# Sliding-window attention scores: 128-key triangles in four quarters of 32 keys on sixteen 32x32 array tiles, in place of two halves of 64 keys on eight 32x64 tiles

## The chip, the cores and the metric

The kernel runs on one core of one Trainium2 chip. The metric is the device time of one execution in microseconds (us). Several executions of each kernel are timed.

## The reference, cut to what matters

```python
def _A_ref(x, wqkv, wo):             # x: 2048 x 1024, 32 heads of 32, window 256
    ...
    scores = jnp.einsum("bhqd,bhkd->bhqk", q, k) * (Dh ** -0.5)
    mask = (idx[:, None] - idx[None, :] >= 0) & (idx[:, None] - idx[None, :] < W)
    scores = jnp.where(mask[None, None], scores, -1e9)
    p = _softmax(scores, axis=-1)
    o = jnp.einsum("bhqk,bhkd->bhqd", p, v)
    ...
h = x + _A_ref(_layernorm(x, axis=-1), A_wqkv, A_wo)
h2 = h + _B_ref(_layernorm(h, axis=-1), B_w1, B_w2)   # dense, SiLU, dense
```

A query sees its own key and the 255 before it. In tiles of 128 keys this gives, for each key tile, one triangle on the diagonal, one full tile, and one triangle at the far end of the window.

## The kernel before

The sequence goes through in four blocks of 512 queries, the heads in eight groups of four. The score work of a block is cut into *bursts*, placed between dense matmuls of the next block (or of the output projection) so that the tensor engine (PE) need not wait (it is busy for 99% of the span). A burst fills the four score banks of PSUM, the memory that PE writes to; ScalarE takes the exponential out of them, GpSimd clears the masked corners, and later PE multiplies by V. An X or Y burst holds, for one group of heads, four triangles (two of the key tile in its middle, one of each of two other key tiles) and one full piece; a C burst holds only full 128-key pieces, which need no mask. A block has 16 X/Y bursts and 4 C bursts.

```python
    def scores_xy(b, g, odd):
        q0 = odd * P
        mid, first, last = odd, odd - 2, odd + 2
        parts = [                                   # key tile, 64-key half, query from, to, bank column
            (mid, 0, q0, q0 + 320, 64), (mid, 1, q0 + 64, q0 + 384, 128),
            (last, 0, q0 + 256, q0 + 384, 384), (first, 1, q0, q0 + 128, 0),
            (first, 0, q0, q0 + 64, 0), (last, 1, q0 + 320, q0 + 384, 448),
        ]
        for step in range(3):
            for hh in range(4):
                for kt, half, qa, qb, col in parts[step * 2:step * 2 + 2]:
                    ...
                    nc.tensor.matmul(
                        sc[hh // 2][half * 64:half * 64 + 64, hh % 2, col:col + qb - qa],
                        lhsT=kT[t // 4][r0:r0 + DH, g, k0:k0 + 64],
                        rhs=qT[b][r0:r0 + DH, g, qa:qb],
                        start=True, stop=True, tile_position=(r0, half * 64),
                    )
        ...                                         # per pair of heads: two exponentials, two selects

    class Stream:
        def __init__(self, b):
            ...
            for g in range(0, G, 2):
                self.bursts += [lambda g=g: scores_c(b, g)]
                self.bursts += [lambda g=g, k=k, o=o: scores_xy(b, g + k, o) for k in range(2) for o in range(2)]
        def between(self, kt):                      # called ahead of each of a block's 192 dense matmuls
            if self.seen * 20 >= self.done * 192:
                self.bursts[self.done]()
                self.done += 1
            ...
```

Each `nc.tensor.matmul` is two instructions of the tensor engine, a weight load and a matmul (the page counts 5859 of each). An X/Y burst has 24 of them, so 48 instructions, in three waves of eight: 320 columns, then 128, then 64 on each 32x64 tile.

The softmax here doesn't subtract the row's maximum and nothing guards it: scores larger than these inputs give would overflow.

## Time and profile before

| | before |
|---|---|
| median of 4 runs | 693.75 us (693.42 to 694.03) |
| span in the profile | 691.9 us |
| PE busy | 99% |
| X/Y burst, cost on PE | 452 ns, 48 of them |
| C burst, cost on PE | 430 ns, 12 of them |
| PE instructions, load and matmul | 11718 |

The cost of a burst is the time from the last dense matmul before it to the first after it, less one dense spacing of 215.5 ns. It is a better figure than "busy", which is 100% in these blocks (58.00 of 58.00 us from 106.00 on), because the records of matmuls overlap: that of a dense one lasts 379 ns, and the next starts after 215.5. The lines that carry these numbers are in the prediction below.

### The profile page before, as it was taken

The numbers are of one execution on the slowest core, as the hardware profiler recorded it, in microseconds if no ns is written. First come the engines' busy times: TensorE is split into PE (matmuls) and PEld (weight loads), VectorE is DVE, ScalarE is ACT, GpSimd is POOL, SyncE is SP. The second block draws the span as 40 slices with busy tenths as digits, with TensorE's granted clock in tenths as the row PEclk, the third lists the DMA queues.
The fourth block names the chain that finished last, engine by engine and source line by source line (L and its number), as shares of the span: only waits on it lengthen the run. The fifth ranks groups of instructions, "written<-read, shape, count | busy, mean of one in ns | idle before, by whom it ended". The sixth has DMA issues, their size and how long they took to land.

```text
span 691.9 us, 13823 instructions
## 1 busy us (share of the span) xinstructions
PE 687.3 (99%) x5859; PEld 330.1 (48%) x5859; DVE 292.5 (42%) x616; ACT 240.8 (35%) x400; POOL 161.8 (23%) x295
## 2 busy tenths in 40 slices
PE   8999999999999999999999999999999999999998
PEld 3444445555555555544444444444444444444445
DVE  6267646744444449543315133343133251333111
ACT  4326656666766676521310033300133100233000
POOL 1007666656666665500000000000000000000000
PEclk9999999999999999999999999999999999999999
DMA  7732231236462999971023410023200023100110
GB/s 243 259 60 72 33 93 54 26 63 174 81 131 18 228 248 276 228 267 46 16 76 109 98 38 1 1 91 70 84 0 1 17 94 94 39 1 1 30 39 24
DMA packets 76462, 60.93 MB, mean 88 GB/s; under 512 B 50288, under 2 KB 60528, under 8 KB 76400
## 3 DMA queue, kind: packets, MB, share of 16 engines
q1 hardware_dynamic: 76256, 59.78, 33.1%
q8 instruction: 46, 0.75, 0.5%
q10 hardware_dynamic: 144, 0.26, 0.1%
q14 instruction: 16, 0.13, 0.1%
HBM read 39.85 MB, written 8.39 MB: 70 GB/s over the span
## 4 chain that ended last, share of the span: by engine, by line
PE 99%; DMA 0%; DVE 0%; issue 0%
PE hacc L615 19%; PE hacc L652 17%; PE acc L250 16%; PE acc L652 10%; PE acc L615 9%; PE acc L240 8%; PE acc L271 7%; PE o_ps L377 4%; PE sc L302 3%; PE hacc L271 1%; PE o_ps L392 1%; PE sc L348 1%; PE sc L328 1%; DMA r_o<-in_A_x_dram 0%; PE tp L218 0%; DVE ln_st L171 0%
## 5 line engine op out<-in xcount | busy, mean ns | idle before, releaser
L368 POOL TENSOR_SCALAR_AFFINE_SELECT r_e<-r_e 128x512 bf16<-128x512 bf16 (+1 forms) x288 | 158.8, 570 | 125.7 <-ACT r_e L357 64.7
L652 PEld LDWEIGHTS <-r_a 128*128 128x128 bf16 x952 | 90.9, 98 | 103.0
L615 PEld LDWEIGHTS <-r_w 128*128 128x128 bf16 x896 | 87.5, 98 | 105.0
L652 PE MATMUL hacc<-r_a 128*128 128x512 bf16 (+2 forms) x616 | 122.5, 360 | 0.0
L615 PE MATMUL hacc<-r_e,r_w 128*128 128x512 bf16 x456 | 100.9, 379 | 0.0
L314 ACT ACTIVATE r_e<-sc 128x768 bf16<-128x768 f32 x96 | 78.2, 814 | 48.3 <-PE sc L302 48.3
L624 ACT ACTIVATE r_n<-hacc 128x512 f32<-128x512 f32 x30 | 17.9, 597 | 178.9 <-PE hacc L615 178.9
L652 PE MATMUL acc<-r_a 128*128 128x512 bf16 x336 | 74.0, 379 | 0.0
L250 PEld LDWEIGHTS <-r_w 128*128 128x128 bf16 x512 | 45.0, 97 | 47.3 <-issue 0.2
L252 DVE CAST r_a<-acc 128x512 bf16<-128x512 f32 x56 | 38.6, 690 | 57.1 <-PE acc L250 56.9
L250 PE MATMUL acc<-r_t,r_w 128*128 128x512 bf16 x256 | 61.7, 379 | 0.0
L250 PE MATMUL acc<-r_w 128*128 128x512 bf16 x256 | 59.9, 379 | 0.0
L271 PE MATMUL acc<-r_o,r_a 128*128 128x512 bf16 x208 | 51.9, 379 | 0.0
L615 PE MATMUL acc<-r_e,r_w 128*128 128x512 bf16 x216 | 49.1, 379 | 0.0
L377 PEld LDWEIGHTS <-r_e 128*128 128x128 bf16 x1152 | 37.8, 96 | 14.2
L357 ACT ACTIVATE r_e<-sc 128x1024 bf16<-128x1024 f32 x36 | 34.9, 1021 | 21.2 <-PE sc L348 20.1
L377 PE MATMUL o_ps<-r_a,r_e 128*128 128x33 bf16 x1152 | 38.3, 178 | 0.0
L667 DVE SCALAR_TENSOR_TENSOR r_t<-hacc,r_t 128x512 bf16<-128x512 f32 (+2 forms) x22 | 14.0, 635 | 56.4 <-PE hacc L652 56.4
L315 ACT ACTIVATE r_e<-sc 128x256 bf16<-128x256 f32 x96 | 37.4, 390 | 0.0
L667 DVE SCALAR_TENSOR_TENSOR r_t<-acc,r_t 128x512 bf16<-128x512 f32 x12 | 8.3, 691 | 64.2 <-PE acc L652 64.2
L625 DVE SCALAR_TENSOR_TENSOR r_a<-r_n,hacc 128x512 bf16<-128x512 f32 x30 | 20.6, 688 | 33.0 <-ACT r_n L624 33.0
L615 PE MATMUL hacc<-r_a,r_w 128*128 128x512 bf16 x144 | 32.9, 379 | 0.0
(75 smaller groups left out, 529.0 us busy)
## 6 DMA issues: line engine op xcount, KB each, us to landing
r_w<-in_B_w_dram SPq DMA_DIRECT2D x8, 896.0 KB, 5.5
r_a<-in_B_w_dram SPq DMA_DIRECT2D x7, 1024.0 KB, 7.8
r_w<-in_A_wqkv_dram SPq DMA_DIRECT2D x6, 1024.0 KB, 8.6
h_dram<-r_t SPq DMA_DIRECT2D x16, 256.0 KB, 3.3
r_t<-h_dram SPq DMA_DIRECT2D x16, 256.0 KB, 2.9
out_dram<-r_t SPq DMA_DIRECT2D x31, 128.0 KB, 1.7
r_o<-in_A_x_dram SPq DMA_DIRECT2D x15, 256.0 KB, 3.6
r_e<-h_dram SPq DMA_DIRECT2D x3, 1024.0 KB, 5.7
```

Source lines behind the costliest of these rows:

```text
L240: nc.tensor.matmul(acc, lhsT=lnT_b[b % 2][:, kt, j * P:(j + 1) * P], rhs=wv[:, kt, c * 512:(c + 1) * 512], start=(kt == 0), stop=(kt == KT ...
L250: nc.tensor.matmul(acc, lhsT=wqk[:, kt, col0:col0 + P], rhs=lnT_b[b % 2][:, kt, :], start=(kt == 0), stop=(kt == KT - 1))
L252: copy(out=(qT, kT)[which][b][:, g, :], in_=acc)
L271: nc.tensor.matmul(acc, lhsT=qT[b][:, g, j * P:(j + 1) * P], rhs=wo[:, g, c * 512:(c + 1) * 512], start=(g == 0), stop=(g == G - 1))
L314: nc.scalar.activation(out=tri[:, :, :, 64:256], in_=both, func=ACT.Exp, scale=scale)
L315: nc.scalar.activation(out=e[:, 1024:1280].rearrange("p (h q) -> p h q", q=P), in_=bank[:, :, 192:320], func=ACT.Exp, scale=scale)
L357: nc.scalar.activation(out=e, in_=sc[pair], func=ACT.Exp, scale=scale)
L368: nc.gpsimd.affine_select(out=dst, in_=src, pattern=[[0, n] for n in dst.shape[1:-1]] + [[sgn, P]], compare_op=ALU.is_ge if upper else ALU ...
L377: nc.tensor.matmul(o_ps[pair][:, qt * 2 + hh, 0:VW], lhsT=chunk_of(i, bank, piece, pair, hh), rhs=v[:, b * 4 + kt, g * 4 + pair * 2 + hh, ...
L615: nc.tensor.matmul(acc, lhsT=w1[:, kt, ft * P:(ft + 1) * P], rhs=ln2T[b][:, kt, :], start=(kt == 0), stop=(kt == KT - 1))
L652: nc.tensor.matmul(acc[:, 0:c1 - c0], lhsT=gT[:, ft, j * P:(j + 1) * P], rhs=w2[ft // 4][:, ft % 4, c0:c1], start=(ft == 0), stop=(ft == F ...
L667: nc.vector.scalar_tensor_tensor(out=t_out[j % 2][:, c0:c1], in0=acc[:, 0:c1 - c0], scalar=0.5, in1=t_in[j % 2][:, c0:c1], op0=ALU.mult, o ...
```

## The change

The intent: cut the triangles into quarters of 32 keys. Two triangles, laid so that one fills the empty half of the other, then need 160 columns of a bank (128 and a skew of 32) in place of 192 (128 and 64), so the two such pairs of a bank leave 64 more columns free. These take half of one full piece, and half of what the C bursts did moves into the X/Y bursts. A block needs 2 C bursts in place of 4, so 18 bursts in place of 20, and each burst has a price beyond its columns: 452 ns for X or Y and 430 for C, where 512 columns of a dense matmul take 215.5. The quarters go to sixteen 32x32 array tiles.

```diff
     def scores_xy(b, g, odd):
-        q0 = odd * P
-        mid, first, last = odd, odd - 2, odd + 2
-        parts = [ ... ]
         for step in range(3):
-            for hh in range(4):
-                for kt, half, qa, qb, col in parts[step * 2:step * 2 + 2]:
+            for k in (range(4), range(4), range(3, -1, -1))[step]:
+                edge = 64 * odd + 32 * (k + 1)
+                kt, q0, col, n = (
+                    (odd, odd * P + 32 * k, edge, 288),
+                    (odd + 2, (odd + 2) * P + 32 * k, edge + 288, 512 - 288 - edge),
+                    (odd - 2, 64 * odd, 0, edge),
+                )[step]
...
+                for hh in range(4):
                     nc.tensor.matmul(
-                        sc[hh // 2][half * 64:half * 64 + 64, hh % 2, col:col + qb - qa],
-                        lhsT=kT[t // 4][r0:r0 + DH, g, k0:k0 + 64],
+                        sc[hh // 2][32 * k:32 * (k + 1), hh % 2, col:col + n],
+                        lhsT=kT[t // 4][r0:r0 + DH, g, k0:k0 + 32],
...
-            nc.scalar.activation(out=tri[:, :, :, 64:256], in_=both, ...)      # 768 elements
+            nc.scalar.activation(out=tri[:, :, :, 96:256], in_=both, ...)      # 640
             nc.scalar.activation(out=e[:, 1024:1280]..., ...)                  # 256
+            nc.scalar.activation(out=c_ring[:, (g + 2) % 4, ...], in_=bank[:, :, half0:half0 + 64], ...)  # 128
...
-    def scores_c(b, g):                   # 16 matmuls of 128 columns, two groups
+    def scores_c(b, g0):                  # 32 matmuls of 64 columns, four groups
...
-            if self.seen * 20 >= self.done * 192:
+            if self.seen * 18 >= self.done * 192:
...
-    obuf = [view(r_n, 512 * i, 4, P) for i in range(3)]
+    obuf = [view(r_n, 512 * i, 4, P) for i in range(2)]
-    c_ring = view(r_e, 0, 3, 4, 256)
+    c_ring = view(r_e, 10240, 4, 4, 256)
```

The rest moves buffers, and gives the attention out in halves of eight units in place of pieces of 8, 8, 5, 6 and 5. An X/Y burst now has 48 matmuls, so 96 instructions, in three waves of sixteen. Each tile still streams 512 columns: 288, then 192 to 96 (X) or 128 to 32 (Y), then the rest.

More of the change, by code (lines that the diff above doesn't have):

```diff
@@ L32 @@
 ]
-SPLIT = [(0, 8), (8, 16), (16, 21), (21, 27), (27, 32)]
 def first_stream(n_groups):
@@ L89 @@
     r_a = big.tile([P, 49664], BF16, name="r_a")
-    r_e = big.tile([P, 13312], BF16, name="r_e")
-    r_n = big.tile([P, 1536], BF16, name="r_n")
+    r_e = big.tile([P, 14336], BF16, name="r_e")
+    r_n = big.tile([P, 1024], BF16, name="r_n")
     ps_tp = tc.tile_pool(name="ps_tp", bufs=1, space=bass.MemoryType.PSUM, reuse_waits="tile")
@@ L126 @@
     ebuf = [view(r_e, 1024 * i, 2, 512) for i in range(12)]
-    c_ring = view(r_e, 0, 3, 4, 256)
-    xy_ring = [r_e[:, 3072 + 1280 * i:3072 + 1280 * (i + 1)] for i in range(8)]
-    obuf = [view(r_n, 512 * i, 4, P) for i in range(3)]
+    c_ring = view(r_e, 10240, 4, 4, 256)
+    xy_ring = [r_e[:, 1280 * i:1280 * (i + 1)] for i in range(8)]
+    obuf = [view(r_n, 512 * i, 4, P) for i in range(2)]
     h_blk = [view(r_a, w2_off + 4096 * 4, 4, D)] + [view(r_e, 8192, 4, D)] * 3
@@ L157 @@
     load_wqkv(0)
-    ident = const.tile([P, P], BF16, name="ident")
-    make_identity(nc, ident[:])
+    ident = view(r_e, 2048, P)
+    make_identity(nc, ident)
     warm = ebuf[0]
@@ L217, in turn_first @@
                 kt = h * 2 + i
-                nc.tensor.transpose(out=tp_ps[h][:, i * P:(i + 1) * P], in_=xt[:, kt * P:(kt + 1) * P], identity=ident[:])
+                nc.tensor.transpose(out=tp_ps[h][:, i * P:(i + 1) * P], in_=xt[:, kt * P:(kt + 1) * P], identity=ident)
             nc.scalar.copy(out=dst[:, h * 2:(h + 1) * 2, j * P:(j + 1) * P],
@@ L280, in chunk_of @@
         if bank == "C":
-            return c_ring[:, (i + 1) % 3, pair * 2 + hh, piece * P:(piece + 1) * P]
+            return c_ring[:, (i + 2) % 4, pair * 2 + hh, piece * P:(piece + 1) * P]
         c0 = 1024 + hh * P if piece == 2 else hh * 512 + (piece - piece // 3) * P
@@ L287, in scores_xy @@
     def scores_xy(b, g, odd):
-        q0 = odd * P
-        mid, first, last = odd, odd - 2, odd + 2
-        parts = [
-            (mid, 0, q0, q0 + 320, 64), (mid, 1, q0 + 64, q0 + 384, 128),
-            (last, 0, q0 + 256, q0 + 384, 384), (first, 1, q0, q0 + 128, 0),
-            (first, 0, q0, q0 + 64, 0), (last, 1, q0 + 320, q0 + 384, 448),
-        ]
-        for step in range(3):
-            for hh in range(4):
-                for kt, half, qa, qb, col in parts[step * 2:step * 2 + 2]:
-                    r0 = hh * DH
-                    t = b * 4 + kt
-                    k0 = (t % 4) * P + half * 64
-                    nc.tensor.matmul(
-                        sc[hh // 2][half * 64:half * 64 + 64, hh % 2, col:col + qb - qa],
-                        lhsT=kT[t // 4][r0:r0 + DH, g, k0:k0 + 64],
-                        rhs=qT[b][r0:r0 + DH, g, qa:qb],
-                        start=True, stop=True, tile_position=(r0, half * 64),
-                    )
@@ L308, in scores_xy @@
-        for pair in range(2):
-            e = xy_ring[((b * G + g) % 2 * 2 + odd) * 2 + pair]
-            tri = e[:, 0:1024].rearrange("p (h c q) -> p h c q", h=2, q=256)
-            bank = sc[pair]
-            both = bank[:, :, 0:192]
-            both = bass.AP(tensor=both.tensor, offset=both.offset, ap=[*both.ap[:2], [320, 2], both.ap[2]])
-            nc.scalar.activation(out=tri[:, :, :, 64:256], in_=both, func=ACT.Exp, scale=scale)
-            nc.scalar.activation(out=e[:, 1024:1280].rearrange("p (h q) -> p h q", q=P), in_=bank[:, :, 192:320], func=ACT.Exp, scale=scale)
-            four = e[:, 0:1024].rearrange("p (c q) -> p c q", q=256)
-            select(four[:, :, 0:P], four[:, :, 64:64 + P], False)
-            select(four[:, :, P:2 * P], four[:, :, P:2 * P], True)
@@ L320, in scores_c @@
-    def scores_c(b, g):
-        s0, s1 = (b * G + g + 1) % 3, (b * G + g + 2) % 3
-        order = (g, g + 1) if s0 < s1 else (g + 1, g)
-        for n, gg in enumerate(order):
-            for m, (kt, q) in enumerate(((-1, 0), (2, 3))):
+        for step in range(3):
+            for k in (range(4), range(4), range(3, -1, -1))[step]:
[5 more added lines that the diff above has]
+                )[step]
@@ L325, in scores_c @@
                 t = b * 4 + kt
+                k0 = (t % 4) * P + 32 * k
                 for hh in range(4):
@@ L328, in scores_c @@
                     nc.tensor.matmul(
-                        sc[hh // 2][:, hh % 2, (n * 2 + m) * P:(n * 2 + m + 1) * P],
-                        lhsT=kT[t // 4][r0:r0 + DH, gg, (t % 4) * P:(t % 4 + 1) * P],
-                        rhs=qT[b][r0:r0 + DH, gg, q * P:(q + 1) * P],
+                        sc[hh // 2][32 * k:32 * (k + 1), hh % 2, col:col + n],
+                        lhsT=kT[t // 4][r0:r0 + DH, g, k0:k0 + 32],
+                        rhs=qT[b][r0:r0 + DH, g, q0:q0 + n],
+                        start=True, stop=True, tile_position=(r0, 32 * k),
+                    )
@@ new lines, in scores_xy @@
+        tri0, full0, half0 = 64 * odd, 64 * odd + 160, 448 * (1 - odd)
+        for pair in range(2):
+            bank = sc[pair]
+            e = xy_ring[((b * G + g) % 2 * 2 + odd) * 2 + pair]
+            tri = e[:, 0:1024].rearrange("p (h c q) -> p h c q", h=2, q=256)
+            both = bank[:, :, tri0:tri0 + 160]
+            both = bass.AP(tensor=both.tensor, offset=both.offset, ap=[*both.ap[:2], [288, 2], both.ap[2]])
+            nc.scalar.activation(out=tri[:, :, :, 96:256], in_=both, func=ACT.Exp, scale=scale)
+            nc.scalar.activation(out=e[:, 1024:1280].rearrange("p (h q) -> p h q", q=P), in_=bank[:, :, full0:full0 + P], func=ACT.Exp, scale=scale)
+            nc.scalar.activation(out=c_ring[:, (g + 2) % 4, pair * 2:pair * 2 + 2, 128 - 64 * odd:192 - 64 * odd],
+                                 in_=bank[:, :, half0:half0 + 64], func=ACT.Exp, scale=scale)
+            four = e[:, 0:1024].rearrange("p (c q) -> p c q", q=256)
+            select(four[:, :, 0:P], four[:, :, 96:96 + P], False)
+            select(four[:, :, P:2 * P], four[:, :, P:2 * P], True)
@@ new lines, in scores_c @@
+    def scores_c(b, g0):
+        for m, (kt, q0) in enumerate(((-1, 0), (2, 3 * P + 64))):
+            t = b * 4 + kt
+            for n in range(4):
+                g = g0 + (n + 2) % 4
+                for hh in range(4):
+                    r0 = hh * DH
+                    nc.tensor.matmul(
+                        sc[hh // 2][:, hh % 2, m * 256 + n * 64:m * 256 + (n + 1) * 64],
+                        lhsT=kT[t // 4][r0:r0 + DH, g, (t % 4) * P:(t % 4 + 1) * P],
+                        rhs=qT[b][r0:r0 + DH, g, q0:q0 + 64],
@@ L332, in scores_c @@
                         start=True, stop=True, tile_position=(r0, 0),
                     )
-        lo, hi = min(s0, s1), max(s0, s1)
         for pair in range(2):
-            nc.scalar.activation(out=c_ring[:, lo:hi + 1:hi - lo, pair * 2:pair * 2 + 2, :],
-                                 in_=sc[pair].rearrange("p h (n q) -> p n h q", q=256), func=ACT.Exp, scale=scale)
+            for m in range(2):
+                nc.scalar.activation(out=c_ring[:, :, pair * 2:pair * 2 + 2, m * 192:m * 192 + 64],
+                                     in_=sc[pair][:, :, m * 256:(m + 1) * 256].rearrange("p h (n q) -> p n h q", q=64),
+                                     func=ACT.Exp, scale=scale)
@@ L405, in attn_norm @@
         nc.vector.tensor_tensor(
-            out=obuf[i % 3][:, :, pair * 64:(pair + 1) * 64].rearrange("p t (h d) -> p t h d", d=DH),
+            out=obuf[i % 2][:, :, pair * 64:(pair + 1) * 64].rearrange("p t (h d) -> p t h d", d=DH),
             in0=o_ps[pair][:, :, 0:DH].rearrange("p (t h) d -> p t h d", h=2),
@@ L413, in attn_transpose, with attn_half @@
         nc.sync.dma_start_transpose(out=qT[b][:, g, :].rearrange("p (t q) -> p t q", q=P),
-                                    in_=obuf[i % 3].rearrange("p t d -> p (t d)"))
-    def attn_piece(b, g, first, last):
-        for k in range(2):
-            a, z = max(first - 16 * k, 0), min(last - 16 * k, 16)
-            if a < z:
-                attn_out(b, g + k, a, z)
-                if z == 16:
-                    late.append(lambda k=k: attn_transpose(b, g + k))
+                                    in_=obuf[i % 2].rearrange("p t d -> p (t d)"))
+    def attn_half(b, g, half):
+        attn_out(b, g, half * 8, half * 8 + 8)
+        if half:
+            late.append(lambda: attn_transpose(b, g))
     class Stream:
         def __init__(self, b):
-            self.b, self.bursts, self.done, self.given, self.seen = b, [], 0, 0, 0
-            for g in range(0, G, 2):
-                self.bursts += [lambda g=g: scores_c(b, g)]
-                self.bursts += [lambda g=g, k=k, o=o: scores_xy(b, g + k, o) for k in range(2) for o in range(2)]
+            self.bursts, self.halves, self.done, self.given, self.seen = [], [], 0, 0, 0
+            for g0 in range(0, G, 4):
+                four = [lambda g=g0 + k, o=o: scores_xy(b, g, o) for k in range(4) for o in range(2)]
+                self.bursts += four[0:2] + [lambda g=g0: scores_c(b, g)] + four[2:]
+                self.halves += [lambda g=g0 + k, o=o: attn_half(b, g, o) for k in range(4) for o in range(2)]
         def between(self, kt):
-            if self.seen * 20 >= self.done * 192:
+            if self.seen * 18 >= self.done * 192:
                 self.bursts[self.done]()
                 self.done += 1
-            if self.seen * 40 >= (self.given * 2 + 1) * 192:
+            if self.seen * 36 >= (self.given * 2 + 1) * 192:
+                if self.given % 9 >= 3:
+                    pending.append(self.halves.pop(0))
                 if pending:
                     pending.pop(0)()
-                coming.append(lambda b=self.b, n=self.given: attn_piece(b, n // 5 * 2, *SPLIT[n % 5]))
-                if len(coming) > 2:
-                    pending.append(coming.pop(0))
+                if self.given % 9 == 8:
+                    pending.extend(self.halves[:2])
+                    del self.halves[:2]
                 self.given += 1
@@ L522 @@
     steps, turns = ln1_steps(2)
-    pending, coming = [], []
+    pending = []
     count = [0, 0]
@@ L599 @@
                 steps.pop(0)()
-    pending += coming
     while steps:
```

## The prediction

The sum came to -2.5 + 0.6 + 0.4 - 0.3 = -1.8 us, so 692.1. From rival B a sum on an assumed 13 ns an instruction came to some 200 ns a burst, about 10 us in all, and so to its 702. The text counts columns at 2.4 a ns (53.3, 133 and 213 ns for 128, 320 and 512). The profile before has this rate: by their records, matmuls of 128 and of 512 columns last 219 and 379 ns (L652), so 384 columns take 160; and dense ones of 512 start 215.5 ns apart. The 2 ns a wave and the 13 ns for the first weights are estimates from it and from the spacings in the text.

> **What bounds the kernel now.** I read the page first, then the stretches of the span by stage, then the timeline around single score bursts, then the trace record by record on the tensor engine.
>
> The page and the stretches say the same thing: the tensor engine (PE) is the bound everywhere. Columns of the stretches: start and end in us, length, then the busy time of each engine with its count of instructions, the granted clock and the DMA share.
>
> ```profile
> PE 687.3 (99%) x5859; PEld 330.1 (48%) x5859; DVE 292.5 (42%) x616; ACT 240.8 (35%) x400; POOL 161.8 (23%) x295
> ...
> PE 99%; DMA 0%; DVE 0%; issue 0%
> ```
>
> ```profile
> 106.00:164.00 58.00, 58.00 (x982) 30.75 (x981) 35.60 (x81) 38.72 (x68) 38.45 (x63) 1.00 0.23 35
> 164.00:224.00 60.00, 60.00 (x1017) 32.02 (x1022) 25.96 (x56) 40.79 (x72) 39.84 (x64) 1.00 0.53 114
> 224.00:288.00 64.00, 64.00 (x1086) 34.27 (x1071) 37.79 (x88) 42.86 (x76) 43.35 (x69) 1.00 0.98 242
> ```
>
> The change touches blocks 1 to 3, about 106 to 291 us. There ScalarE (ACT) is busy for two thirds of the time and GpSimd (POOL) likewise, neither on the path. So what counts is how long PE needs for one score burst, and how many bursts there are. "Busy" cannot tell this, as PE is busy 100% whatever happens. The timeline can: columns are start, length, engine, line, operation, then the count.
>
> ```profile
> 141.24 1.24 PE L250 MATMUL acc<-r_w 128*128 128x512 bf16 x5
> ...
> 142.41 0.29 PEld L302 LDWEIGHTS <-r_a 32*64 32x64 bf16 x24 [0.42 <-issue]
> 142.41 0.43 PE L302 MATMUL sc<-r_a 32*64 32x320 bf16 x24
> 142.77 0.55 PEld L250 LDWEIGHTS <-r_w 128*128 128x128 bf16 x4
> 142.77 1.04 PE L250 MATMUL acc<-r_w 128*128 128x512 bf16 x4
> ```
>
> The dense matmuls start 0.2155 us apart (from the records), so after five that begin at 141.24 the sixth would start at 142.32. It starts at 142.77: a burst of X or Y scores costs 0.45 us. The records split it: 93 ns from the end of the dense stream to the first score matmul, 239 ns from the first score matmul to the last, 120 ns from there to the next dense one. 47 of the 48 such bursts cost 452 or 453 ns. The same reckoning gives 429 to 431 ns for all twelve C bursts, for example this one (dense from 135.41, four of them, so due at 136.27, back at 136.70):
>
> ```profile
> 135.41 1.02 PE L250 MATMUL acc<-r_w 128*128 128x512 bf16 x4
> ...
> 136.36 0.40 PE L328 MATMUL sc<-r_a 32*128 32x128 bf16 x16
> ...
> 136.70 1.25 PE L250 MATMUL acc<-r_w 128*128 128x512 bf16 x5
> ```
>
> One burst, at 114.76, waits for ScalarE to empty the score banks and costs 745 ns, 0.29 us too much; note its weight loads cut in two groups.
>
> ```profile
> 114.76 0.11 PEld L302 LDWEIGHTS <-r_a 32*64 32x64 bf16 x5 [0.42 <-issue]
> 114.76 0.72 PE L302 MATMUL sc<-r_a 32*64 32x320 bf16 x24
> 115.07 0.28 PEld L302 LDWEIGHTS <-r_a 32*64 32x64 bf16 x19 [0.20 <-issue]
> ```
>
> The attention pieces (P times V) cost 25.4 ns a matmul and no entry or exit.
>
> [...]of a burst's 452 ns about 93 are the way in and, by the records, some 90 the way out after the last column. This fixed part is what a dropped burst saves. [...]Here eight tiles of 32x64 start 3.3 ns apart; sixteen are not in this trace. [...]An X/Y burst now is 48 (24 loads, 24 matmuls)[...]. [...]The trace has 814 ns for 768 elements and 390 for 256: 0.828 ns an element plus 178.
>
> **The change, part by part.** *C bursts:* the full 128-key pieces of the C bank lose their middle columns to the X and Y bursts, which gain 64 columns of room. So a block has 2 C bursts in place of 4. Each new one has 32 matmuls of 64 columns in place of 16 of 128, the same 512 columns on each of four row tiles. Eight waves in place of four cost some 2 ns each more (128 columns now come 55 to 57 ns apart, 53.3 of it columns at the full clock), so I take 440 ns. Before 12 x 430 = 5.16 us, after 6 x 440 = 2.64 us: **minus 2.5 us**.
>
> *X/Y bursts:* still 16 a block, with 48 matmuls on sixteen tiles. Per tile the columns are 288 + (224 - edge) + edge = 512; before, 320 + 128 + 64 = 512. So the streaming time, 213 ns, does not fall: quarters only make the triangle's blocks tighter, which buys the 64 columns. What grows is the stagger, sixteen starts in place of eight: 8 x 3.3 = 26 ns more. What shrinks is the wait for the first weights: the first wave now lasts 160 ns for 320 columns (133 ns), so 27 ns go to loading 64 columns; for 32 columns I take 13. Net 26 - 13 = 13 ns, at 48 bursts: **plus 0.6 us**.
>
> *ScalarE:* per burst and pair of heads it now has 768 and 256 elements, then 640, 256 and 128: 708 + 390 + 284 ns from the line above. Six instructions sum to 2.76 us; now four sum to 2.41 and take 2.06 on the clock (139.93 to 141.99), an overlap of 0.116 each, so 2.18 us after. A block's period per burst goes from 57.7 / 20 = 2.9 us to about 3.3, so it hides. Between a C burst and the next one, though, there are ten dense matmuls and no attention piece: 2.155 + 0.44 = 2.6 us from start to start, while the banks come free about 0.2 + 0.36 + 2.06 + 0.05 = 2.67 us after the burst's start (spans and waits as in the bursts of before). That is an estimated wait of 0.07 us six times, **plus 0.4 us**; the 0.29 us wait at 114.76 goes, as X and Y bursts are now 10 or 11 dense matmuls and an attention piece apart: **minus 0.3**.
>
> *POOL, attention, buffers:* the selects are the same 192 of the same size, at a longer period; the 1152 attention matmuls are the same, at no switch cost. Each half of a group comes at least 1.5 periods, some 4.9 us, after its last burst; exponentials and selects need about 3 for the first pair of heads. Output buffers go from three to two. A buffer is written again three slots, 9.9 us, after its last write; its transposing DMA lands 2.3 to 6.2 us after issue. Near 285 us the queue is full of other transposes, so a wait below 1 us could appear there. I count zero.
>
> Sum: -2.5 + 0.6 + 0.4 - 0.3 = -1.8 us, so 692.1; I put the middle at **692.5**, as the risks lie on the slow side.
>
> **The rivals.** *Rival A, four streams of columns don't run at full rate.* The sixteen tiles need four different moving streams per row group, now two. [...]At half rate each burst costs 213 ns more: 48 x 0.213 = 10.2 us, so about 702. [...]I give it 17%.
>
> *Rival B, feeding.* [...]A block now averages 28.8 ns an instruction over 57.7 us, and after the change about 20; the trace only shows that the feed is at least that good. [...]Against: the 1.65 ns between two instructions inside a burst shows how fast the array takes them. I give it 15%.
>
> *Rival C, ScalarE or POOL becomes the bound* through 50% more activations. 2.18 us in a period of 3.3 speaks against; if each burst waited 0.1 us it would be 54 x 0.1 = 5 us, so 697. 5%.
>
> **Range and chances.** The plain sum gives 692.1 with about 1 us either way; A or B alone puts it at 702. Eight in ten: 691.0 to 702.5. Faster by over 2% (below 680) would need more than all the bursts' fixed cost, 1%. Slower by over 2% (above 707.7) needs 290 ns more in every X/Y burst, A and B together: 4%.
>
> **What would show it.** In the new timeline an X/Y burst's cost, reckoned as above, should be 455 to 480 ns, with the sixteen first starts within 55 ns; 650 or more means A or B. A shows as a first wave of about 250 ns and even spacing; B as a first wave of 135 to 150 ns, then a gap before the third. C bursts: 430 to 450 ns, two a block. Weight loads split in two groups by a gap mean a wait for ScalarE. The attention matmuls must stay at 25.4 ns; if not, POOL or the two output buffers hold them.

## The result, and the profile after

The changed kernel takes **702.48 us** (701.53 to 703.15, 4 runs) against 693.75 (693.42 to 694.03, 4 runs). The ratio, the mean time of one kernel's runs over that of the other's of the same rounds (so not quite the ratio of these medians), is 1.0125, 95% interval 1.0108 to 1.0143. That is 1.25% slower, which is clear of noise. Its results are correct. It spreads more than the kernel before: 1.6 us from fastest to slowest, against 0.6.

The page after still shows PE as the whole chain, with a little "issue", time in which PE waited for nothing the profile shows:

```profile
PE 684.6 (98%) x6906; PEld 338.7 (48%) x7011; DVE 292.1 (42%) x616; ACT 236.0 (34%) x496; POOL 161.2 (23%) x295
...
PE 97%; issue 2%; DVE 0%; DMA 0%
```

The timeline around one X burst (start, length, engine, line, operation, count):

```profile
146.07 0.81 PE L251 MATMUL acc<-r_w 128*128 128x512 bf16 x3
...
146.81 0.53 PEld L302 LDWEIGHTS <-r_a 32*32 32x32 bf16 x48 [0.42 <-issue]
146.81 0.63 PE L302 MATMUL sc<-r_a 32*32 32x288 bf16 x48
...
147.37 0.55 PEld L251 LDWEIGHTS <-r_w 128*128 128x128 bf16 x4
147.37 0.82 PE L251 MATMUL acc<-r_w 128*128 128x512 bf16 x2
```

Three dense matmuls from 146.07, so the fourth is due at 146.72; it starts at 147.37. The burst costs 0.65 us in place of 0.45. (In many bursts after, the record of the first dense matmul is missing, though its weight load is there; those were read from the load.) All X bursts cost 651 ns and all Y bursts 677 to 679, but for two X bursts, of 700 and 1118 ns, that waited. A C burst:

```profile
143.68 0.59 PE L251 MATMUL acc<-r_w 128*128 128x512 bf16 x2
144.20 0.29 PEld L330 LDWEIGHTS <-r_a 32*128 32x128 bf16 x32 [0.42 <-issue]
144.21 0.41 PE L330 MATMUL sc<-r_a 32*128 32x64 bf16 x32
144.55 0.55 PEld L251 LDWEIGHTS <-r_w 128*128 128x128 bf16 x4
```

Two dense matmuls from 143.68, the next due at 144.11, back at 144.55: 441 ns, as all six are.

What fills the 651 ns? The stretches below count only the X burst's own line; look at the weight loads (PEld), whose records are 87 ns long:

```profile
146.81:147.09 0.28, 0.28 (x32) 0.28 (x33) 1.00 0.88 207
147.09:147.13 0.04, 0.04 (x32) 0.00 (x0) 1.00 1.29 294
147.13:147.26 0.13, 0.13 (x41) 0.12 (x15) 1.00 1.29 293
```

33 of 48 loads come in the first stretch; then there are none at all; then the last 15. Record by record: counted from the burst's first load, the first wave's sixteen matmuls start within 50 ns of each other in most bursts (3.3 ns apart; 58 in this one), the second wave starts at 135 ns and its last matmul at about 185 (194 in this one), and then nothing starts until **320 ns**. From there loads and matmuls come alternately, one each 4.17 ns, the last matmul at 445. The 33rd load, the 65th instruction of the burst, is the last that comes in time. The tiles are free long before: in this burst the third wave's first tile ends its 96 columns, at 2.4 a ns, 40 ns after it began them, near 224 ns.

Where the time went, from the two profiles (spans 691.9 and 700.1, a difference of 8.2 us):

| term | us |
|---|---|
| X/Y bursts, 48: 22.03 to 32.43 | +10.40 |
| C bursts, 12 to 6: 5.17 to 2.65 | -2.52 |
| two stalls of PE outside bursts (175.04 and 279.27, see the run "shift") | +0.97 |
| earlier start of the score stage (50.57 to 50.08; something in the start-up, not looked into) | -0.50 |
| sum | +8.35 |

The terms sum to 0.17 us more than the spans differ by; that rest was not traced. From the first matmul of the dense half on, the two traces take the same 404.92 us. The attention matmuls stay at 25.4 ns apart.

### The profile page after: what moved, and what is told of

Its sections match the earlier page's. It is cut to its first block, busy times and chain, and to the rows that moved or that the text cites. A ratio compares the mean times of both kernels' runs of the same rounds, so it can differ in the third digit from the quotient of the medians.

```text
span 700.1 us, 16094 instructions
## 1 busy us (share of the span) xinstructions
PE 684.6 (98%) x6906; PEld 338.7 (48%) x7011; DVE 292.1 (42%) x616; ACT 236.0 (34%) x496; POOL 161.2 (23%) x295
## 4 chain that ended last, share of the span: by engine, by line
PE 97%; issue 2%; DVE 0%; DMA 0%
PE hacc L617 18%; PE hacc L654 17%; PE acc L251 16%; PE acc L654 10%; PE acc L617 9%; PE acc L241 8%; PE acc L272 6%; PE o_ps L380 4%; PE sc L302 4%; PE hacc L272 1%; PE o_ps L395 1%; PE sc L351 1%; DMA r_o<-in_A_x_dram 0%; PE tp L219 0%; PE sc L330 0%
## 5 line engine op out<-in xcount | busy, mean ns | idle before, releaser
L315 ACT ACTIVATE r_e<-sc 128x640 bf16<-128x640 f32 x96 | 68.6, 714 | 64.8 <-PE sc L302 57.2
L251 PE MATMUL acc<-r_t,r_w 128*128 128x512 bf16 x237 | 58.0, 379 | 1.8 <-issue 1.3
L251 PE MATMUL acc<-r_w 128*128 128x512 bf16 x241 | 57.1, 379 | 1.6 <-issue 1.3
L272 PE MATMUL acc<-r_o,r_a 128*128 128x512 bf16 x190 | 47.9, 379 | 2.3 <-issue 1.9
L380 PEld LDWEIGHTS <-r_e 128*128 128x128 bf16 x1152 | 36.1, 96 | 11.8 <-issue 0.5
L380 PE MATMUL o_ps<-r_a,r_e 128*128 128x33 bf16 x1152 | 36.6, 178 | 0.4 <-issue 0.4
L302 PEld LDWEIGHTS <-r_a 32*32 32x32 bf16 x2304 | 22.9, 88 | 23.3 <-issue 20.7
```

The lines of the kernel that those rows point to most:

```text
L251: nc.tensor.matmul(acc, lhsT=wqk[:, kt, col0:col0 + P], rhs=lnT_b[b % 2][:, kt, :], start=(kt == 0), stop=(kt == KT - 1))
L272: nc.tensor.matmul(acc, lhsT=qT[b][:, g, j * P:(j + 1) * P], rhs=wo[:, g, c * 512:(c + 1) * 512], start=(g == 0), stop=(g == G - 1))
L302: nc.tensor.matmul(sc[hh // 2][32 * k:32 * (k + 1), hh % 2, col:col + n], lhsT=kT[t // 4][r0:r0 + DH, g, k0:k0 + 32], rhs=qT[b][r0:r0 + DH ...
L315: nc.scalar.activation(out=tri[:, :, :, 96:256], in_=both, func=ACT.Exp, scale=scale)
L380: nc.tensor.matmul(o_ps[pair][:, qt * 2 + hh, 0:VW], lhsT=chunk_of(i, bank, piece, pair, hh), rhs=v[:, b * 4 + kt, g * 4 + pair * 2 + hh, ...
```

## The experiments

**Theory F (feed).** The count of a burst's instructions makes the gap, whatever tiles they run on: up to about the 65th they start in time, and later ones from about 320 ns after the burst's first, one each 4.2 ns, as in the profile after. **Rival Q (quarter tiles).** Something about 32x32 tiles makes the third wave slow by itself: its weights, the mode, or four streams of columns for each row of tiles. The four streams are already answered by the trace: from the first wave's start to the second's start on the same tile there are 133 ns, which is 288 columns at 2.4 per ns (120; the rate agrees with "y_order" below, where 64 columns are 26 ns) and 13 that are left for the first weights. So four streams run at the rate of the other matmuls. What was open was whether the count of instructions or the shape of the tile makes the gap.

### s64, s68, s96: the kernel before, longer bursts

```diff
         # at the end of scores_xy, tiles still 32x64
+        for n in range(8):        # 10 in s68, 24 in s96
+            hh = n // 2 % 4
+            kt, half, qa, qb, col = parts[4 + n % 2]
+            ...                   # the same product again, 32 of its columns
```

The repeats write the same values again, so the result stays correct.

> The kernel before, with the 32x64 tiles kept and eight 32-column score matmuls repeated at the end of each X/Y burst: 64 instructions a burst. [...]F expects no gap here: last matmul 265 to 295 ns after the first, a burst costs 465 to 500 ns. Rival Q (quarter tiles: the third weights of a 32x32 tile are slow in themselves) expects the same.

> As s64 with ten repeats: 68 instructions a burst, still 32x64 tiles. F expects a step: the 33rd matmul not before 318 ns after the burst's start, the last at about 328, a burst 525 to 545 ns. Q expects no step: each of two matmuls more costs 4 to 50 ns in all, the 33rd starts as soon as its tile is free, below 300 ns.

> As s64 with 24 repeats: 96 instructions a burst on 32x64 tiles, as many as the changed kernel has on 32x32. F expects the changed kernel's pattern: matmuls 33 to 48 from 320 ns on, 8.3 ns apart, the last at about 445, a burst 640 to 660 ns. Q expects six even waves, the last matmul at 285 to 400 ns and a burst of 485 to 600 ns.

One burst of each, first s64, then s68, then s96 (L314 is the repeats):

```profile
185.01 0.29 PEld L302 LDWEIGHTS <-r_a 32*64 32x64 bf16 x24 [0.42 <-issue]
...
185.23 0.13 PEld L314 LDWEIGHTS <-r_a 32*64 32x64 bf16 x8
...
185.39 0.76 PEld L240 LDWEIGHTS <-r_t 128*128 128x128 bf16 x5
```

```profile
186.97 0.29 PEld L302 LDWEIGHTS <-r_a 32*64 32x64 bf16 x24 [0.42 <-issue]
...
187.19 0.23 PEld L314 LDWEIGHTS <-r_a 32*64 32x64 bf16 x10
...
187.45 0.55 PEld L240 LDWEIGHTS <-r_t 128*128 128x128 bf16 x4
```

```profile
189.50 0.29 PEld L302 LDWEIGHTS <-r_a 32*64 32x64 bf16 x24 [0.42 <-issue]
...
189.72 0.35 PEld L314 LDWEIGHTS <-r_a 32*64 32x64 bf16 x24
...
190.10 0.55 PEld L240 LDWEIGHTS <-r_t 128*128 128x128 bf16 x4
```

From the burst's first load to the dense matmuls' first load: 0.38, 0.48 and 0.60 us.

| | instructions | 32nd matmul starts | 33rd | last | cost of a burst | one run, us |
|---|---|---|---|---|---|---|
| s64 | 64 | 269 ns | - | 269 ns | 472 ns | 694.88 |
| s68 | 68 | 269 ns | 346 ns | 355 ns | 576 ns | 699.82 |
| s96 | 96 | 269 ns | 347 ns | 472 ns | 692 ns | 705.33 |

Eight matmuls more cost 20 ns; **two more than that cost 104**. The step is there on the old tile shape, so rival Q falls. The times, each of one run beside a run of the kernel before at 693.75, go with it: 48 times 20 ns is 0.9 us (measured 1.1), 48 times 124 is 5.9 (measured 6.1), 48 times 240 is 11.5 (measured 11.6).

Three expectations missed, all on the low side: the 33rd matmul came at 346 ns and not at 320, as in the changed kernel, and the bursts cost 576 ns in s68 (525 to 545 expected) and 692 in s96 (640 to 660). The records explain the 26 ns, which is most of the missing cost, and sharpen the theory. In the changed kernel the first matmul's record ends at 293 ns (288 columns), here at 319 (320 columns, and weights of 64). Both times the 66th instruction comes **27 ns after the recorded end of the burst's first matmul**. A burst of the changed kernel at 115.34 us says the same by itself: its third matmul had to wait for ScalarE and started at 71 ns, not at 9, with its record ending at 349. Four late instructions came from 320 on, and then there was a hole until 376, again 27 ns after that end. What the late ones wait for is not in the trace; what it shows is this distance from the end of a record. F in its sharper form expects the late instructions 27 ns after the first matmul's recorded end, in any burst that is long enough to have some. (The profiler models the ends of matmuls; that the wait follows the first matmul's length is tested in "short_first".)

### split: 64 and 32 instructions in place of 96

```diff
+            if self.seen * 18 >= self.done * 192:
+                self.bursts[self.done]()                        # waves 1 and 2
+                self.tail_at = self.seen + 2
+                ...
+            elif self.seen == self.tail_at:
+                self.bursts[self.done - 1](range(2, 3))         # wave 3, two dense matmuls later
```

> The changed kernel with the third wave of each X/Y burst moved two dense matmuls later: 64 and 32 instructions in place of 96, same tiles, same columns, one more way in and out. F expects the third wave's sixteen matmuls to start within 60 ns of each other (3.3 ns apart, as the first wave), first part about 420 ns, second 260 to 310, together about 700 against 651 to 678 now, so the kernel 1 to 4 us slower than the changed one. Q expects the third wave to stay at 8.3 ns a matmul, 125 ns.

```profile
147.73 0.21 PEld L302 LDWEIGHTS <-r_a 32*32 32x32 bf16 x32 [0.42 <-issue]
147.73 0.39 PE L302 MATMUL sc<-r_a 32*32 32x288 bf16 x32
...
148.59 0.14 PEld L302 LDWEIGHTS <-r_a 32*32 32x32 bf16 x16 [0.42 <-issue]
148.60 0.23 PE L302 MATMUL sc<-r_a 32*32 32x128 bf16 x16
```

The third wave's sixteen matmuls now start within 50 ns, on the very tiles on which they took 125. In a burst of 32 instructions they are as quick as the first wave; this settles Q for the quarter tiles too. But a second way in and out costs what the gap did: from the last dense matmul before to the first after, less three dense spacings, 682 to 692 ns for a plain X burst and 696 to 699 for a plain Y burst. Some 14 bursts cost more, mostly 771 to 776, because their second pair of heads waited for ScalarE to empty the banks. One run took 704.14 us, 1.7 above the changed kernel's median, within the 1 to 4 expected.

### short_first: the same 96 instructions, short matmuls ahead

```diff
-        for step in range(3):
-            for k in (range(4), range(4), range(3, -1, -1))[step]:
+        up, down = range(4), range(3, -1, -1)
+        for piece in (1, 0, 2) if odd else (2, 0, 1):           # shortest piece, middle, the other
+            for k in down if odd else up:
```

> The changed kernel with the pieces of each X/Y burst in another order, the same 48 matmuls and columns: shortest piece first (32, 64, 96, 128 columns), then the 288-column middle, then the rest, longest first. Theory F in its sharper form[...] expects matmul 33 at 205 to 225 ns after the start, as the first matmul now ends near 186, the last at 330 to 350, a burst 550 to 580 ns in place of 651 and 678, and the kernel near 697.5 us. If the late matmuls come at a fixed 320 ns after the burst's start, the last starts at 445 and a burst costs about 670, the kernel near 702.5.

```profile
183.30 1.02 PE L241 MATMUL acc<-r_w,r_t 128*128 128x512 bf16 x4
...
184.25 0.42 PEld L303 LDWEIGHTS <-r_a 32*32 32x32 bf16 x48 [0.42 <-issue]
...
184.73 0.82 PE L241 MATMUL acc<-r_w,r_t 128*128 128x512 bf16 x3
```

The loads take 0.42 us in place of 0.53. The 33rd matmul starts at 212 ns (expected 205 to 225), the last at 337, and a burst costs 571 ns (median of 48) in place of 651 and 678, with the same work in another order. The first matmul's record ends at 186 ns, so the late ones again come some 27 ns after it. A fixed delay of 320 ns is refuted: the late ones start at 212 ns in place of 320, and the end of the first matmul's record moved from 293 to 186. The kernel takes 698.51 us (697.93 to 699.09, 4 runs), ratio to the kernel before 1.0068 (1.0051 to 1.0085): nearly half of the loss is back. (Two stalls of the kind looked at under "shift" stand in this profile too.)

### hybrid: 64 instructions, two shapes of tile

```diff
+        for step in range(2):                                   # outer pieces: sixteen 32x64
+            for hh in range(4):
+                for half in range(2):
+                    edge = 64 * odd + 64 * half + 32
+                    ...                                         # some columns too many for one quarter
+        for k in range(4):                                      # then the middle: sixteen 32x32,
+            ...                                                 # which overwrites those
```

> The changed kernel with 64 instructions in an X/Y burst in place of 96, same results: the two outer pieces as sixteen 32x64 matmuls first, then the middle as sixteen 32x32 that overwrite what the wider ones wrote too much. F expects no gap from feeding. If going from 32x64 to 32x32 drains the array as going from 128x128 does (93 ns), a burst costs 600 to 630 ns and the kernel about 699; if it does not, 500 to 530 ns and about 694.5. Below 504 ns a burst would make it faster than the kernel before.

```profile
184.91 0.15 PEld L301 LDWEIGHTS <-r_a 32*64 32x64 bf16 x16 [0.42 <-issue]
184.91 0.32 PE L301 MATMUL sc<-r_a 32*64 32x192 bf16 x16
...
185.16 0.14 PEld L313 LDWEIGHTS <-r_a 32*32 32x32 bf16 x16
185.16 0.34 PE L313 MATMUL sc<-r_a 32*32 32x288 bf16 x16
...
185.43 0.82 PE L241 MATMUL acc<-r_w,r_t 128*128 128x512 bf16 x3
```

No gap as in s68: the sixteen quarter loads come within 50 ns. But going from one tile shape to the other inside the burst costs time: by the columns, the halves end near 158 ns, and the first quarter starts at 249 to 252, 91 to 95 ns later, as on the way in from the dense matmuls (93). (This wait is what the expectation calls a drain; the traces show its length alone.) A burst costs 617 ns, the kernel 699.06 us (698.43 to 699.57, 4 runs), ratio 1.0074 (1.0059 to 1.0089). Expected were 600 to 630 ns and about 699. A way to keep the quarters' room without the long burst exists, but this wait eats it.

### y_order: what the 27 ns between X and Y bursts are

```diff
+            piece = (0, 2, 1)[step] if odd else step
-            for k in (range(4), range(4), range(3, -1, -1))[step]:
+            for k in (range(4), range(4), range(3, -1, -1))[piece]:
```

> The changed kernel with the second and third pieces of the Y bursts exchanged, so that the late matmuls of a Y burst have 128, 96, 64, 32 columns as those of an X burst do, in place of 192, 160, 128, 96. If the late matmuls' own columns lie bare at the burst's end, Y bursts fall from 678 to 651 ns (64 columns, 26.7 ns) and the kernel by 24 x 0.027 = 0.6 us. If the end of a burst is set by something else, they stay at 678.

Y bursts fall to 652 ns, level with X. One run took 701.83 us (693.52 for the kernel before beside it); 0.6 us is within the spread of the changed kernel's runs, so only the burst's cost shows it. The late matmuls' own columns do lie bare at the end: 64 of them made 26 ns (26.7 expected).

### shift: the rarer stalls

Some profiles have holes of 0.4 to 1.3 us in PE in the middle of dense, attention or score work, each in one place. In the profile after there are three, and one of them, at 249.45, makes an X burst cost 1118 ns in place of 651. They belong to no wait of an engine for another that the trace shows.

```diff
+    for i in range(20):                              # 40 tensor instructions more, at the start
+        nc.tensor.matmul(..., rhs=warm[:, 0, 0:8], start=True, stop=True)
     for i in range(11):
```

> The changed kernel with twenty tiny warm-up matmuls (40 tensor instructions) more at its start, to see what the rarer stalls of 0.4 to 1.3 us are that fall on a tensor instruction in the middle of dense, attention or score work. In four kernels they fall on instruction numbers 4796, 8124 and 9404 of the engine, all 188 more than a multiple of 256. [...]If they come from a wait of those instructions (a buffer, a select), they move with the program to numbers 228 over a multiple. X/Y bursts stay at 651 and 678 ns.

If the stalls go with the count of instructions from the engine's start, they again fall on numbers that are 188 over a multiple of 256, now other instructions of the program.

The numbers of the instruction after each hole (two for each weight load counted before it, from the engine's start):

| kernel | us into the span: number (gap in ns) |
|---|---|
| changed | 175.04: 4796 (396); 249.45: 8124 (482); 279.27: 9404 (600) |
| short_first | 173.77: 4796 (621); 275.89: 9404 (1278) |
| y_order | 175.28: 4796 (435); 273.14: 9148 (401); 279.33: 9404 (992) |
| s96 | 177.25: 4796 (462) |
| split | 281.51: 9404 (729) |
| shift | 174.91: 4796 (734); 266.96: 8892 (860); 286.10: 9660 (940) |

The worst of "shift", in a burst that then cost 1582 ns:

```profile
285.14 0.11 PEld L304 LDWEIGHTS <-r_a 32*32 32x32 bf16 x7 [0.42 <-issue]
285.14 0.31 PE L304 MATMUL sc<-r_a 32*32 32x288 bf16 x6
286.10 0.60 PE L304 MATMUL sc<-r_a 32*32 32x288 bf16 x42 [0.65 <-issue]
```

Every number is 188 more than a multiple of 256, with the program moved by 40 as without. (s64, s68, short_first and hybrid also pause for 0.43 to 0.54 us, start to start, at the first load of the dense half. That is one fixed instruction of the program, and it is not counted here.) So these stalls go with the count of instructions, not with the instructions they fall on. X and Y bursts stayed at 651 and 678 ns; the run took 703.43 us.

The pages also list a DMA queue that the profiler names "instruction" (transfers, MB, share), first before, then after:

```profile
q8 instruction: 46, 0.75, 0.5%
```

```profile
q8 instruction: 55, 0.90, 0.6%
```

46 and 55 are the 11718 and 14022 loads and matmuls divided by 256 and rounded up. Put beside the numbers at 188 over a multiple in order, the first transfer beside number 444, each of the 13 holes of the table ends 1.22 to 1.47 us after its transfer has landed; in the profile after 1.37, 1.33 and 1.26. In the kernels without a hole at such a number, every transfer landed earlier: 3.19 us or more ahead of its instruction in the kernel before, 2.13 or more in s64, s68 and hybrid. (Four other numbers, in short_first and split, came as near, at 1.35 to 1.47 us, with a smaller hole or none.) The traces show this nearness in time. That one causes the other is not shown, nor is what sets the times of the transfers.

The kernel before has no hole above 0.33 us there. The changed one has more instructions: 14022 loads and matmuls in place of 11718, all of the difference in blocks 1 to 3. One to three holes a profile, of 0.4 to 1.3 us and only partly at the same places, could also make the wider spread of its times; no run here tests that.

None of the eight runs beats the kernel before, so there is no better version to offer.

## Why the prediction was right or wrong, point by point

The time, 702.48 us, lies in the stated range by 0.02 us, and two of the four runs (703.05 and 703.15) lie outside. That is luck: the range was stretched to hold rival A or B alone, at 702. The middle, 692.5, was wrong, and wrong in direction: the plain sum said 1.8 us faster, and it is 8.7 slower.

- **C bursts: right.** Predicted 440 ns and minus 2.5 us; measured 441 and minus 2.52.
- **X/Y bursts: this is the term of the sum that failed.** Predicted plus 13 ns a burst, plus 0.6 us; measured plus 199 (X) and 225 (Y) ns, plus 10.2 us for 48 plain bursts. (The 10.40 of the table has the stall of 0.47 and the wait of 0.05 in it, and lacks the old wait of 0.29.) Its parts were right: the stagger of sixteen starts is 50 ns, and the first wave's 133 ns, less 120 for 288 columns, leave 13 for the first weights. The step that failed is the overlap: the sum let all 96 instructions start in time, and the last 31 came only from 320 ns on, after the record of the burst's first matmul had ended at 293. What it left out, and had put to the rivals at 15%, is rival B.
- **Rival B, feeding: its sign is what the trace has:** a first wave of 135 to 150 ns (133 measured) and then a gap before the third. The size was right (some 200 ns a burst, 702 us) by luck, as its arithmetic was not: it assumed slow but steady instructions, 13 ns each. The late ones come 4.17 ns apart, which is quicker, and yet they cost that much, because the first of them starts only at 320 ns.
- **Rival A, four streams not at full rate: refuted** by the same first wave, 288 columns in 133 ns.
- **Rival C, ScalarE as the bound: refuted.** The three activations of a pair of heads take 714, 398 and 305 ns, a little more than the 708, 390 and 284 reckoned, and fit: in the profile after one X/Y burst waits for the banks, by 48 ns (at 115.34).
- **Waits after C bursts, plus 0.4 us: once in six times,** the 48 ns just named (0.05 us in all); the other five bursts behind a C burst cost the plain 651 or 652 ns. The wait of 0.29 us at 114.76 went, as predicted.
- **Selects and attention matmuls unchanged: right,** 25.4 ns apart. The two output buffers cost nothing that can be seen.
- **Not foreseen:** the stalls at instruction numbers 188 over a multiple of 256, about 1.4 us in the profile after (0.97 outside bursts and 0.47 in the burst at 248.55).
- **Slips in the sums that changed nothing:** a block lasts 60.3 us from its first burst to that of the next (106.22, 166.50, 226.79), not 57.7, so a burst's period was 3.0 us and became 3.5, and an instruction took 29 to 30 ns and now takes 22. 693.75 less 1.8 is 691.95, not 692.1. And 290 ns more a burst leads from the kernel before to the 2% mark; from the plain sum it takes 325.

## What to carry to other kernels

Count the instructions of a burst of small matmuls, not only its columns: here, in a burst set between dense matmuls, the first 64 loads and matmuls came at up to 3.3 ns a pair (s64, hybrid and split have no gap), and with more (the changed kernel, s68, s96, short_first) the next ones came some 27 ns after the recorded end of the burst's first matmul. The finer cut of the array doubled the instructions, and had to save more than the 199 to 225 ns a burst that this cost; it saved 2.5 us of C bursts in all. Where a long burst can't be avoided, the order of its matmuls is worth a try: with the shortest first, and no long ones last, this one cost 571 ns in place of 651 and 678.
